# Long convolution and 2-D Fourier filter on one core: the 4096 points split as 128 by 32 in place of 64 by 64

## The chip, the cores and the metric

The kernel runs on one core of one Trainium2 chip. The core has five engines that each work through their own list of instructions: TensorE (PE in the profile; its weight loads are PEld), VectorE (DVE), ScalarE (ACT), GpSimd (POOL), and SyncE (SP), which here issues all DMAs. The metric is device time in microseconds of one execution; lower is better. Three runs of the kernel before gave 575.78, 577.08 and 578.83 us, median 577.08.

## What is computed

The input `x` has 2048 positions and 640 channels. Branch a is a long convolution: a kernel `K` of 2048 taps per channel is made from 128 complex modes and applied through transforms of 4096 points. Branch b is a two-dimensional real transform, a product with `w`, and the way back. A sigmoid gate per position mixes both.

```python
def reference(A_u, A_log_A_real, A_A_imag, A_C_real, A_C_imag, A_log_dt, A_D_skip, B_x, B_w_r, B_w_i, gate_w):
    # a: u = A_u, L = 2048
    dt = exp(log_dt)
    A = -exp(log_A_real) + 1j * A_imag
    C = (C_real + 1j * C_imag) * dt[:, None]
    P = exp((A * dt[:, None])[:, :, None] * arange(L))
    K = 2.0 * einsum("dn,dnl->dl", C, P).real
    y = irfft(rfft(u_t, 2 * L) * rfft(K, 2 * L))[:, :, :L]
    a = y.transpose + u * D_skip
    # b
    b = irfft2(rfft2(x) * (w_r + 1j * w_i))
    g = sigmoid((x * gate_w).sum(-1))
    return g * a + (1 - g) * b
```

## The kernel before, in words

**Transforms in two steps.** A transform over time is split: position n = a + 64 b, frequency in two parts as well. The first step sums over b with a small table of cosines and sines, the second over a with a table per first frequency. `POS_K` lists the 33 first frequencies that a real input needs, `NP` their number; `T.e1` is the first table, `T.w2` the second. The 640 channels are handled as four groups c of 160. All data is float32; a float32 matmul of the program is two matmul instructions in the trace.

**Where things stand.** `body` calls the parts in turn: `columns_head` and `columns` (transform u along time, write it to `u_d` in DRAM, and sum the gates), `params` (prepare the modes on DVE, ACT and POOL), `responses` (make K), `spectral` (branch b on the even time frequencies in `u_d`, result to `s3e_d`), and `convolution` (transform K, multiply by `u_d`, transform back, mix with branch b, write out).

- `stage1` is the first transform. Eight channel blocks are one step: 32 matmuls in which the data block is the weight and the table `T.e1` moves, 64 columns each, into a pair of PSUM banks; then two copies of 128x512 into `t1`, both on ACT or one of them on DVE. Groups are handled in two parts of 24 and 16 blocks (`HALVES`), so a group takes five steps; `columns` and `convolution` have four groups each.
- `stage2` is the second transform: for each first frequency two matmuls with 128x64 weights from `T.w2` and 160 moving columns from `t1`.
- The gate in `columns`: POOL builds a spread copy of the gate weights (L696), PE multiplies it with u (L704), ACT copies, and at the end DVE reduces (L719).
- `columns` writes second-transform results through `ut` to `u_d` (copies L715, half on ACT, half on DVE).
- `responses` has 40 tiles of 16 channels, in batches of five. `mags` makes exponentials (PE L919, ACT L920), `turned` sines (PE L931, ACT L932), `phases` the products on POOL (L941) and DVE (L946 to L949), and `kgen` the taps: 64 matmul instructions per tile, 128x32 weights, 64 moving columns (L962). Every two tiles go through ACT to `k_d`.
- `spectral` runs a software pipeline over nine blocks: `front` (L772 is its first DVE step), `transposes`, `channels`, `filt`, `back1`, `back2` (L856).
- `convolution`: `first` runs `stage1` on K from `k_d`. `unit` takes two pairs of frequencies: `stage2` into PSUM, two DVE products with u (L1015, L1016), two DVE sums (L1017, L1018), the inverse second step on PE (L1028), one ACT copy into `s3` (L1031). `final` sums the even branch through PE and ACT (L1043, L1054), turns `s3` by DVE's 32x32 block transposition (L1056), sums it on PE and mixes on DVE (L1059). Its buffers lie on those of `params` and `responses`, so group 0's transform of K starts when the last tile of K is made.

**What sets the order.** Nothing is issued directly: `Engine` records each call in `Plan` with its dependences, and `order` (a planner with modelled durations) chooses one order for all engines. Its weights are in `OPT`: a bias per part ("A" columns, "P" parameters, "K" responses, "F" spectral, "C" convolution) and thresholds. Each engine then works through its list in that order and waits where an operand is not ready. SP's list of DMAs is in order too: a DMA that waits for its data holds back those behind it.

Of the kernel before, what the change touches and what calls it, by code (L numbers as in the profile page):

```python
# [10 lines left out]
F32 = mybir.dt.float32  # L11
# [3 lines left out]
ALU = mybir.AluOpType  # L15
# [10 lines left out]
NP = 33  # L26
# [17 lines left out]
A_ORDER = [*range(31, -1, -1), *range(32, 64)]  # L44


def _tables():

    b = np.arange(32)
    co = np.array([np.cos(2 * np.pi * k * b / 64) for k in POS_K])  # L50
    si = np.array([-np.sin(2 * np.pi * k * b / 64) * (k not in (0, 32)) for k in POS_K])


    kr = np.stack([co, si], 1)
    kr[K0, 1] = co[32]
    e1 = np.zeros((2, 2, 2, 32, 2, 32))
    for r in range(2):
        e1[:, :, r, :, r, :] = kr[:32].transpose(1, 2, 0)[:, None]
    e1 = e1.reshape(2, 128, 64)

    e3 = np.tile(kr[:32].swapaxes(0, 1).reshape(64, 32), (2, 1))
    kr = kr[:32].reshape(64, 32)
    e3e = np.zeros((2, 32, 2, 2, 32))
    for x in range(2):
        e3e[:, :, x, x, :] = kr[32:64]
    one = np.tile(np.eye(32), (4, 1))
    c1 = np.concatenate([
        e1[0], e1[1], e3, e3e.reshape(128, 64), np.eye(128), one,
        np.repeat([-1.0, 1.0], 64)[:, None], np.repeat([1.0, -1.0], 64)[:, None],
        np.full((128, 1), HALF_PI)], 1)  # L70
# [1040 lines left out]
```

## Time and profile before

| what | value |
| --- | --- |
| runs of the kernel | 575.78, 577.08, 578.83 us |
| the profiled execution | 575.73 us |
| its span in the profile | 573.9 us |
| mean granted clock of TensorE | 0.944 |
| DMA moved | 79.44 MB, mean 138 GB/s |
| instructions in the trace | 21303 |

The span is what the profiler saw between the first and the last instruction; 1.8 us of the execution's own time lie around it. Busy time is the union of an engine's instructions. Matmuls are pipelined, so the duration of one contains filling and draining; what many cost together is read from a run of them on the timeline (start of the run, length of the run, count). The chain that ended last covers only the last ten us here, so the span is read by stretches of it.

### The profile page before, as it was taken

The numbers are of one execution on the slowest core, as the hardware profiler recorded it, in microseconds if no ns is written. First come the engines' busy times: TensorE is split into PE (matmuls) and PEld (weight loads), VectorE is DVE, ScalarE is ACT, GpSimd is POOL, SyncE is SP. The second block draws the span as 40 slices with busy tenths as digits, with TensorE's granted clock in tenths as the row PEclk, the third lists the DMA queues.
The fourth block names the chain that finished last, engine by engine and source line by source line (L and its number), as shares of the span: only waits on it lengthen the run. The fifth ranks groups of instructions, "written<-read, shape, count | busy, mean of one in ns | idle before, by whom it ended". The sixth has DMA issues, their size and how long they took to land. (4 is left out here: it accounts for less than half of the span.)

```text
span 573.9 us, 21303 instructions
## 1 busy us (share of the span) xinstructions
PE 489.1 (85%) x9428; PEld 339.9 (59%) x9428; DVE 423.5 (74%) x763; ACT 356.3 (62%) x553; POOL 178.8 (31%) x159
## 2 busy tenths in 40 slices
PE   4858998978899988999999998786798889979973
PEld 3647775655675755665765765464666666655530
DVE  7298533766999999999899886650736868928975
ACT  3443349579598796787888869653274544753550
POOL 2156412613824738355456470900000000000000
PEclk9798999988899999899999999985899999989996
DMA  8825871863106051443221202168556342452522
GB/s 317 300 95 198 297 276 47 272 223 102 48 21 201 11 163 42 128 157 98 94 66 49 74 32 74 44 237 320 145 188 170 106 146 88 153 139 74 148 104 91
DMA packets 36773, 79.44 MB, mean 138 GB/s; under 512 B 3717, under 2 KB 21001, under 8 KB 35913
## 3 DMA queue, kind: packets, MB, share of 16 engines
q1 hardware_dynamic: 36680, 78.08, 41.6%
q8 instruction: 74, 1.21, 0.9%
q14 instruction: 19, 0.15, 0.1%
HBM read 49.40 MB, written 28.67 MB: 136 GB/s over the span
## 5 line engine op out<-in xcount | busy, mean ns | idle before, releaser
L941 POOL TENSOR_TENSOR sb<-sb 128x512 f32<-128x512 f32 x80 | 105.9, 1351 | 79.2 <-ACT sb L932 66.9
L658 PE MATMUL ps<-sb 128*64 128x160 f32 x1056 | 98.3, 324 | 9.3 <-DVE sb L1016 3.6
L658 PEld LDWEIGHTS ps<-sb 128*64 128x64 f32 x1056 | 75.0, 141 | 32.2 <-issue 12.0
L931 PE MATMUL ps<-sb 52*128 52x512 bf16 x480 | 69.0, 381 | 13.8 <-DVE sb L949 8.0
L645 PE MATMUL ps<-sb 64*64 64x64 f32 x2560 | 56.0, 237 | 28.0 <-ACT sb L648 9.7
L1031 ACT COPY sb<-ps 128x640 f32<-128x640 f32 x32 | 42.0, 1312 | 55.3 <-PE ps L1028 47.8
L648 ACT COPY sb<-ps 128x512 f32<-128x512 f32 x65 | 45.3, 770 | 45.9 <-PE ps L645 45.2
L645 PEld LDWEIGHTS ps<-sb 64*64 64x64 f32 x2560 | 49.3, 149 | 39.1 <-ACT sb L648 13.5
L1015 DVE TENSOR_TENSOR sb<-ps,sb 128x640 f32<-128x640 f32 (+1 forms) x36 | 28.0, 779 | 49.8 <-PE ps L658 49.6
L920 ACT ACTIVATE sb<-ps 128x1024 f32<-128x1024 f32 (+1 forms) x80 | 62.2, 836 | 2.2 <-PE ps L919 2.1
L1028 PE MATMUL ps<-sb 64*64 64x160 f32 x1024 | 49.1, 310 | 9.2 <-issue 3.3
L1028 PEld LDWEIGHTS ps<-sb 64*64 64x64 f32 x1024 | 36.7, 136 | 25.3 <-issue 9.9
L932 ACT ACTIVATE ps<-ps 128x1024 f32<-128x1024 f32 x40 | 40.5, 1013 | 17.4 <-PE ps L931 13.2
L949 DVE TENSOR_TENSOR sb<-sb,ps 128x512 f32<-128x512 f32 x80 | 51.1, 679 | 0.0
L932 ACT ACTIVATE sb<-ps 128x1024 f32<-128x1024 f32 x40 | 41.3, 1031 | 14.0 <-PE ps L931 12.9
L931 PEld LDWEIGHTS <-sb 52*128 52x128 bf16 x480 | 25.1, 95 | 40.6 <-issue 24.4
L755 PE MATMUL ps<-sb 128*128 128x161 f32 (+3 forms) x280 | 48.3, 314 | 0.2
L962 PEld LDWEIGHTS ps<-sb 128*32 128x32 f32 x2560 | 39.4, 112 | 12.0 <-issue 8.6
L962 PE MATMUL ps<-sb 128*32 128x64 f32 x2560 | 45.9, 225 | 0.0
L946 DVE SCALAR_TENSOR_TENSOR sb<-sb,ps 128x512 f32<-128x512 f32 x40 | 27.3, 683 | 24.4 <-ACT ps L932 23.9
L755 PEld LDWEIGHTS ps<-sb 128*128 128x128 f32 (+1 forms) x280 | 39.5, 188 | 9.3 <-issue 7.2
L1043 PE MATMUL ps<-sb 64*32 64x480 f32 (+1 forms) x384 | 31.9, 709 | 6.5 <-DVE sb L1056 5.1
(129 smaller groups left out, 776.9 us busy)
## 6 DMA issues: line engine op xcount, KB each, us to landing
sb<-u_d SPq DMA_DIRECT2D x24, 640.0 KB
u_d<-sb SPq DMA_DIRECT2D x32, 320.0 KB
sb<-in_w_l SPq DMA_DIRECT2D x8, 642.0 KB
k_d<-sb SPq DMA_DIRECT2D x20, 256.0 KB
s3e_d<-sb SPq DMA_DIRECT2D x16, 320.0 KB
sb<-s3e_d SPq DMA_DIRECT2D x8, 640.0 KB
out<-sb SPq DMA_DIRECT2D x3, 1280.0 KB
sb<-k_d SPq DMA_DIRECT2D x4, 768.0 KB
```

Of the source, the lines that this page charges most:

```text
L645: T.P.matmul(p[64 * ri:64 * ri + 64, h, 64 * j:64 * j + 64], src(i + j)[l], T.e1[ri][l], start=True, stop=True)
L648: copies[h](t1v[:, h, q:q + 2 * n], p[:, h, 0:64 * n].rearrange("p (q x y) -> p q x y", x=16, y=2))
L658: T.P.matmul(p[64 * j:64 * j + 64, i, 160 * ri:160 * ri + 160], T.w2[:, x, 64 * ri:64 * ri + 64], t1[:, x // 2 if x < 32 else K0 // 2, :, ...
L755: P.matmul(p[:, 161 * i:161 * i + n], lhs(i, part), tab(i)[part][0], start=i == 0, stop=False)
L920: u = S.activation(ef[:, :, c:c + n], p[:, :, :n], AF.Exp)
L931: P.matmul(p[:, h, :], st.pp[l, zz], turns[l, v, s], start=s == 0, stop=s == 2)
L932: u = S.activation(p if o is None else o, p if o is None else p.rearrange("p h (v c) -> p h v c", v=2), AF.Sin, scale=TWO_PI)
L941: G.tensor_tensor(out=y[:, v], in0=e[:, :, 64:96], in1=sc[:, 1 - v], op=ALU.mult)
L949: V.tensor_tensor(out=xh[:, 0, h].rearrange("p d (y j) -> p d y j", y=2), in0=eh[:, h, :, 0:64].rearrange("p d (y j) -> p d y j", y=2), in ...
L962: P.matmul(st.pb[32 * r:32 * r + 32, o, :], y[:, ri, 4 * qq + JR[r], :], x[:, ri, 4 * qq + JR[r], :], start=t % 2 + qq + 1 - ri == 0, stop ...
L1028: P.matmul(q[x:x + 64, j, 160 * i:160 * i + 160], w3[l, pr + i, ri, x:x + 64], t2[l, ri, i, :], start=ri + i == 0, stop=ri + i == 2)
L1031: S.copy(s3[:, :, 2 * pr:2 * pr + 4].rearrange("p d (i j) -> p j i d", j=2), q[:, :, 0:320].rearrange("p j (i d) -> p j i d", i=2))
```

## The change

The split is now n = a + 32 b with 64 values of b and 65 first frequencies in place of 33.

- First transform: the table `T.e1` is the weight and 16 blocks of data move through it, 512 columns at a time, two matmuls per step. The outcome has frequency along partitions and position along columns; DVE turns it in 32x32 blocks straight out of the PSUM pair into `t1` (L643). The copies are gone. A group still takes five steps.
- Second transform: tables of 64x32, eight places of the PE array in place of two.
- The gate sums are 16 DVE passes over a second copy of u, laid out by position (`u_n`, eight DMAs), each with an accumulated output (L709).
- `kgen` makes 32-column taps: twice as many matmuls, half as wide.
- `back2` and the inverse step in `unit` use smaller tiles; `finish` uses fewer, larger ones. The sums in `unit` move from DVE to POOL. The PSUM banks of `convolution` are shared out anew: one pair for `stage2`, four banks for the inverse, one pair for `final`.
- In `columns` the copies to `ut` are all ACT's for groups 1 to 3.
- `params` takes two more DVE steps (the phase is brought back into one turn).
- Besides small corrections of its modelled durations, the planner has in `OPT` a bias per function and engine instead of five.

```diff
-NP = 33
+NP = 65
-OPT = {"bias": {"A": 9e3, "F": 20e3, "K": -19.5e3, "C": -14e3, "P": -1500.0}, "hold": 100.0, ...
+OPT = {"bias": {"back1.DVE": -104576, "channels.ACT": -19089, ..., "A": -213990}, "slack": ...
-HALVES = ((0, 24), (24, 16))
+HALVES = ((0, 48), (48, 32))
...
-    V.scalar_tensor_tensor(out=ph, in0=th, scalar=-0.5, in1=ph, op0=ALU.mult, op1=ALU.add)
+    V.scalar_tensor_tensor(out=ph, in0=th, scalar=1008.0, in1=ph, op0=ALU.mult, op1=ALU.add)
+    V.tensor_scalar(out=y, in0=ph, scalar1=MAGIC, scalar2=MAGIC, op0=ALU.add, op1=ALU.subtract)
+    V.tensor_tensor(out=ph, in0=ph, in1=y, op=ALU.subtract)
...
-def stage1(T, pair, src, q0, nq, t1, copies):
+def stage1(T, pair, src, q0, nq, t1):
+    t1v = t1.rearrange("p (h q) k -> p h (q k)", h=2)
+    for i in range(0, nq, 16):
+        p = pair()
+        with block(T.R):
+            for h in range(2):
+                l = slice(64 * h, 64 * h + 64)
+                T.P.matmul(p[:, h], T.e1[l], src(i)[l], start=True, stop=True)
+        q = 32 * (q0 + i)
+        T.V.transpose(t1v[:, :, q:q + 512], p)
         yield
-def stage2(T, p, t1, pr, i):
+def stage2(T, ps, t1, g):
+    with block(T.R):
+        for ri in range(2):
+            o = slice(160 * ri, 160 * ri + 160)
...
+            for j in range(4):
+                for s in range(2):
+                    l = slice(64 * s, 64 * s + 64)
+                    T.P.matmul(ps[s][32 * j:32 * j + 32, o], T.w2[l, 4 * g + j, 32 * ri:32 * ri + 32], t1[l, :, 4 * g + j], start=True, stop=True)
...
-                (V.tensor_copy if i else S.copy)(ut[:nl, i], src)
+                (S.copy, V.tensor_copy if c == 0 else S.copy)[i](ut[:nl, i], ps[i][:nl, 0:320])
...
+    for i in range(0, 16, 2):
+        un = T.un()
+        Y.dma_start(un, A["u_n"][:, i:i + 2])
+        for j in range(2):
+            V.scalar_tensor_tensor(out=T.gx, in0=un[:, j], scalar=1.0, in1=T.gw, op0=ALU.mult, op1=ALU.mult, accum_out=T.gate[:, 0, i + j:i + j + 1])
...
+                for e, p in enumerate(pp):
+                    P.matmul(p[64 * hf:64 * hf + 64, 0:320], w3[64 * e:64 * e + 64, kk, :], st.qq[j][64 * e:64 * e + 64, 320 * hf:320 * hf + 320], start=True, stop=True)
...
-            for qq in range(4):
-                o = 4 * (t % 2) + qq
+            for q in range(8):
                 for ri in (1, 0):
-                    for r in (0, 1, 2, 3):
-                        P.matmul(st.pb[32 * r:32 * r + 32, o, :], y[:, ri, 4 * qq + JR[r], :], x[:, ri, 4 * qq + JR[r], :],
+                    for h in range(2):
+                        for s in range(2):
+                            o = 64 * h + 32 * s
+                            P.matmul(st.pb[o:o + 32, 8 * (t % 2) + q, :], x[:, ri, 8 * h + q, 32 * s:32 * s + 32], y[:, ri, 8 * h + q, :],
...
-    rings = [(Banks(R, [5], 2), Banks(R, [3], 2))] * 2 + [(Banks(R, [6], 2), Banks(R, [2, 4], 2))] * 2
+    fin, two, four = Banks(R, [0], 2), Banks(R, [2], 2), Banks(R, [4], 4)
+    begin = Banks(R, [3, 5], 2)
...
-        V.tensor_tensor(out=t2[:nl, 0, :n], in0=ma[:nl, :n, 0], in1=ma[:nl, :n, 1], op=ALU.subtract)
-        V.tensor_tensor(out=t2[:nl, 1, :n], in0=mb[:nl, :n, 0], in1=mb[:nl, :n, 1], op=ALU.add)
+        G.tensor_tensor(out=t2[:nl, 0, :n], in0=ma[:nl, :n, 0], in1=ma[:nl, :n, 1], op=ALU.subtract)
+        G.tensor_tensor(out=t2[:nl, 1, :n], in0=mb[:nl, :n, 0], in1=mb[:nl, :n, 1], op=ALU.add)
...
+                for j in range(4):
+                    for s in range(2):
+                        l, o = slice(32 * j, 32 * j + 32), slice(64 * s, 64 * s + 64)
...
+                        P.matmul(q[o, j, 0:160], w3[l, 2 * g + s, ri, :], t2[l, ri, s, :], start=ri == 0, stop=ri == 1)
+        S.copy(s3[:, :, 4 * g:4 * g + 4].rearrange("p d j -> p j d"), q[:, :, 0:160])
...
                 for s in range(2):
-                    for x in range(2):
-                        for j in range(2):
-                            l, o = slice(64 * j, 64 * j + 64), 64 * x + 32 * s
-                            P.matmul(p[o:o + 32, j], w(l, x), src(l, x, 8 * s + a, n), start=True, stop=True)
+                    for j in range(2):
+                        P.matmul(p[64 * s:64 * s + 64, j], w(j), src(j, 8 * s + a, n), start=True, stop=True)
```

The planner's order moves with it. First the head of SP's list, before and after. Names: `in_cr_l`, `in_ci_l`, `in_la_l`, `in_ai_l`, `in_ld_l`, `in_t_pc`, `in_t_r` belong to the parameters, `in_t_c` and `in_t_w` are the transform tables, `in_u_l` and `in_u_n` the two copies of u, `in_gw_l` the gate weights; behind them stand the sizes.

```order
L548 DMA sb<-in_cr_l 128x640
L548 DMA sb<-in_ci_l 128x640
L671 DMA sb<-in_u_l 128x512
L517 DMA sb<-in_t_c 128x128
L671 DMA sb<-in_u_l 128x1024 x2
L519 DMA sb<-in_t_c 128x259
L677 DMA sb<-in_gw_l 128x160
L691 DMA sb<-in_t_w 128x768 x2
L694 DMA sb<-in_u_l 128x1536
```

```order
L545 DMA sb<-in_cr_l 128x640
L545 DMA sb<-in_ci_l 128x640
L542 DMA sb<-in_ld_l 128x5
L545 DMA sb<-in_ai_l 128x640
L545 DMA sb<-in_la_l 128x640
L549 DMA sb<-in_t_pc 128x640
L546 DMA sb<-in_t_r 128x3840
L549 DMA sb<-in_t_pc 128x640 x3
L552 DMA sb<-in_ds_l 1x320 x2
L692 DMA sb<-in_u_l 128x1536
L689 DMA sb<-in_t_w 128x704 x3
L707 DMA sb<-in_u_n 128x1280
```

All parameters moved ahead of u and of the tables; `in_t_c` with the first table, third to fourth place before, now comes behind the second load of `in_u_n`.

Second, DVE's list where the convolution begins, before and after. L847 and L831 are the last step of the spectral part, L967 the skip term of a finished block of K, L1015 and L1016 (L999 and L1000 after) the two products of a unit.

```order
L847 TENSOR_TENSOR sb<-sb 128x2x160
L967 TENSOR_TENSOR sb<-sb 128x8
L1015 TENSOR_TENSOR sb<-ps,sb 128x640
L1016 TENSOR_TENSOR sb<-ps,sb 128x640
L1017 TENSOR_TENSOR sb<-sb 128x320
L1018 TENSOR_TENSOR sb<-sb 128x320
```

```order
L643 STREAM_TRANSPOSE sb<-ps 128x2x512 x4
L827 TENSOR_TENSOR sb<-ps,sb 64x161 x4
L643 STREAM_TRANSPOSE sb<-ps 128x2x512
L831 TENSOR_TENSOR sb<-sb 64x2x160
L999 TENSOR_TENSOR sb<-ps,sb 32x320
L1000 TENSOR_TENSOR sb<-ps,sb 32x320
L999 TENSOR_TENSOR sb<-ps,sb 128x640
L1000 TENSOR_TENSOR sb<-ps,sb 128x640
```

The five transpositions of group 0 stand between the end of K and the first product, the last spectral steps among them, and the sums are gone from this list. Further up, DVE's list has ten tiles of `phases` ahead of the first step of `front`, five before.

More of the change, by code (lines that the diff above doesn't have):

```diff
@@ L279, in call @@
             out = k["out"] if "out" in k else a[0]
-            ins = [x for x in aps if x is not out]
+            ins = [x for x in aps if x is not out and x is not k.get("accum_out")]
             n = max(x.free_size() for x in (out, *ins) if x.space != DRAM)
@@ L553, in params @@
     V.memset(T.dsk, 0.0)
[L554 to L555 removed]
+    for r in range(2):
+        Y.dma_start(T.dsk[64 * r + 31:64 * r + 32], A["ds_l"][r:r + 1])
     x, kf, r, h = t5(), t5(), t5(), t5()
@@ L694, in columns @@
                 Y.dma_start(T.us[-1][:, 0:n], A["u_l"][c + 1, :, q0:q0 + n])
-            zz = T.az()[:, 0:n]
-            G.tensor_tensor(out=zz, in0=T.one.unsqueeze(1).broadcast_to([128, n, 32]),
-                            in1=T.gw[:, c, q0:q0 + n].unsqueeze(2).broadcast_to([128, n, 32]), op=ALU.mult)
-            for _ in stage1(T, pair, lambda q: u[:, q, :], q0, n, t1, (S.copy, V.tensor_copy if c else S.copy)):
-                pass
-            p = bank()[:, 0:64]
-            with block(R):
-                for q in range(n):
-                    x = 32 * (q % 4)
-                    P.matmul(p[x:x + 32], zz[:, q, :], u[:, q, :], start=q < 4, stop=q >= n - 4)
@@ L718, in columns @@
-    p = bank()[:, 0:64]
-    V.tensor_reduce(out=T.lr, in_=T.lg.rearrange("p x a -> p a x"), axis=mybir.AxisListType.X, op=ALU.add)
-    with block(R):
-        for r in range(4):
-            P.matmul(p[32 * r:32 * r + 32], T.one, T.lr, start=True, stop=True)
-    for r in range(4):
-        l, a = slice(32 * r, 32 * r + 32), 8 * r
-        V.tensor_copy(T.gate[l, 0, 0:8], p[l, 31 - a:23 - a if r < 3 else None:-1])
-        V.tensor_copy(T.gate[l, 0, 8:16], p[l, 32 + a:40 + a])
+            for _ in stage1(T, pair, lambda i: u[:, i:i + 16, :].rearrange("p q a -> p (q a)"), q0, n, t1):
+                pass
@@ L873, in spectral @@
         if old:
-            for j in range(old.nl // 64):
+            for j in range(old.nj):
                 back2(old, n - 2, j)
@@ L881, in spectral @@
                 front(n + 1, sts[n + 1])
-            for j in range(prv.nl // 64):
+            for j in range(prv.nj):
                 back1(prv, j)
```

288 lines of the change are left out of this document (128 added, 160 removed).

## The prediction

> **What bounds the kernel now.** I read the first part of the page (busy time of each engine), then the table of stretches. Its columns are: stretch and length in us; busy us and instructions of PE, PEld, DVE, ACT and POOL; granted clock; DMA share and GB/s. I cut the span where the timeline shows the work change.
>
> ```profile
> PE 489.1 (85%) x9428; PEld 339.9 (59%) x9428; DVE 423.5 (74%) x763; ACT 356.3 (62%) x553; POOL 178.8 (31%) x159
> core 0: us, PE busy (x) PEld busy (x) DVE busy (x) ACT busy (x) POOL busy (x), PEclk, DMA share, GB/s
> 0.00:98.00 98.00, 74.15 (x2034) 61.31 (x2034) 56.02 (x92) 44.75 (x80) 32.70 (x27) 0.93 0.63 220
> 98.00:121.00 23.00, 22.08 (x508) 15.27 (x497) 16.27 (x31) 15.57 (x24) 11.45 (x10) 1.00 0.75 250
> 121.00:383.00 262.00, 238.58 (x3650) 158.68 (x3646) 228.13 (x414) 205.85 (x313) 134.05 (x123) 0.96 0.28 90
> 383.00:401.00 18.00, 12.79 (x340) 10.08 (x340) 0.60 (x1) 7.95 (x12) 0.57 (x1) 0.70 0.92 349
> 401.00:552.00 151.00, 133.51 (x2801) 92.05 (x2802) 109.70 (x204) 75.83 (x111) 0.00 (x0) 0.97 0.45 130
> 552.00:574.00 22.00, 8.00 (x112) 2.48 (x111) 12.79 (x26) 6.33 (x16) 0.00 (x0) 0.78 0.30 120
> 250.00:300.00 50.00, 48.23 (x802) 32.91 (x801) 46.95 (x79) 41.35 (x63) 27.18 (x26) 1.00 0.32 99
> ```
>
> No single engine bounds the whole program. I name the rows A to F. In C, where the kernel responses (K) and the two-dimensional filter (F) run together, DVE is busy 228 of 262 us, and 94% in its steady part (last row). In E, the convolution, PE leads with 133.5 of 151 us, DVE has 109.7, POOL nothing. In D almost nobody works. In A, DVE is busy 56 of 98 us. So a change can win in A, D and E by freeing PE or ordering work better; C follows DVE's load.
>
> The starts that I use (start us, duration us, engine, line, what; in brackets the idle time before and who ended it):
>
> ```profile
> 3.76 0.49 DVE L594 TENSOR_SCALAR sb<-sb 128x640 int32<-128x640 int32 x1 [2.20 <-DMA sb<-in_cr_l]
> 69.97 0.35 SPq L583 DMA_DIRECT2D pp_d<-sb  x1
> 83.35 1.28 ACT L920 ACT_TABLE_LOAD   x1 [1.08 <-PE ps L919]
> 97.64 0.69 DVE L946 SCALAR_TENSOR_TENSOR sb<-sb,ps 128x512 f32<-128x512 f32 x1 [0.96 <-ACT ps L932]
> 102.47 0.69 DVE L946 SCALAR_TENSOR_TENSOR sb<-sb,ps 128x512 f32<-128x512 f32 x1 [0.96 <-ACT ps L932]
> 120.90 0.83 DVE L772 TENSOR_TENSOR sb<-sb 128x640 f32<-128x640 f32 x1 [1.15 <-DMA sb<-u_d]
> 390.85 2.41 PE L645 MATMUL ps<-sb 64*64 64x64 f32 x64 [1.11 <-ACT sb L648]
> 401.05 0.82 DVE L1015 TENSOR_TENSOR sb<-ps,sb 128x640 f32<-128x640 f32 x1 [17.45 <-PE ps L658]
> ```
>
> DVE could work from 3.76, but K's first step on DVE stands at 97.64 and F's first at 120.90. Alone, K takes 4.8 us a tile (97.64 to 102.47). In D, DVE idles 17.45 us while PE and ACT hand one PSUM pair to and fro (L645 waits for L648).
>
> **The change, part by part.** Groups (line, engine, operation, count, busy us, mean ns, idle before):
>
> ```profile
> L946 DVE SCALAR_TENSOR_TENSOR sb<-sb,ps 128x512 f32<-128x512 f32 x40 | 27.3, 683 | 24.4 <-ACT ps L932 23.9 <-PE ps L962 0.3
> L947 DVE TENSOR_TENSOR sb<-sb,ps 128x512 f32<-128x512 f32 x40 | 27.1, 678 | 0.0
> L949 DVE TENSOR_TENSOR sb<-sb,ps 128x512 f32<-128x512 f32 x80 | 51.1, 679 | 0.0
> L648 ACT COPY sb<-ps 128x512 f32<-128x512 f32 x65 | 45.3, 770 | 45.9 <-PE ps L645 45.2 <-PE ps L658 0.7
> L648 DVE COPY sb<-ps 128x512 f32<-128x512 f32 x15 | 10.3, 693 | 13.9 <-PE ps L645 13.8
> L715 DVE COPY sb<-ps 128x320 f32<-128x320 f32 x32 | 15.3, 488 | 22.6 <-PE ps L658 19.3 <-issue 2.4 <-ACT sb L715 0.7
> L1056 DVE STREAM_TRANSPOSE sb<-sb 128x1024 f32<-128x1024 f32 x20 | 23.8, 1222 | 2.7 <-ACT sb L1031 2.7
> L1017 DVE TENSOR_TENSOR sb<-sb 128x320 f32<-128x320 f32 (+1 forms) x36 | 16.6, 461 | 1.7 <-PE ps L1028 1.6
> L1018 DVE TENSOR_TENSOR sb<-sb 128x320 f32<-128x320 f32 (+1 forms) x36 | 16.7, 466 | 0.2
> L608 DVE SCALAR_TENSOR_TENSOR sb<-sb 128x640 f32<-128x640 f32 x1 | 0.8, 818 | 0.0
> L621 DVE SCALAR_TENSOR_TENSOR sb<-sb 128x640 f32<-128x640 f32 x1 | 2.0, 2011 | 0.0
> L846 POOL TENSOR_TENSOR sb<-sb 128x320 f32<-128x320 f32 x17 | 16.5, 970 | 40.7 <-DVE sb L843 40.7
> L856 PE MATMUL ps<-sb 128*128 128x320 f32 x68 | 25.9, 488 | 0.8 <-DVE sb L815 0.6
> ```
>
> And on PE, weight loads and matmuls of small tiles, with one unit of the convolution:
>
> ```profile
> 251.39 2.01 PE L962 MATMUL ps<-sb 128*32 128x64 f32 x128
> 419.67 1.04 PE L1043 MATMUL ps<-sb 64*32 64x480 f32 x16
> 545.09 0.18 PEld L1043 LDWEIGHTS ps<-sb 64*32 64x32 f32 x16 [0.24 <-DVE sb L1017]
> 409.46 0.82 DVE L1016 TENSOR_TENSOR sb<-ps,sb 128x640 f32<-128x640 f32 x1
> 410.33 1.38 PE L658 MATMUL ps<-sb 128*64 128x160 f32 x16 [0.38 <-DVE sb L1016]
> 411.64 1.33 PE L1028 MATMUL ps<-sb 64*64 64x160 f32 x32
> 411.83 0.82 DVE L1015 TENSOR_TENSOR sb<-ps,sb 128x640 f32<-128x640 f32 x1 [0.76 <-PE ps L658]
> 300.13 2.55 POOL L941 TENSOR_TENSOR sb<-sb 128x512 f32<-128x512 f32 x2
> 300.68 1.27 DVE L949 TENSOR_TENSOR sb<-sb,ps 128x512 f32<-128x512 f32 x2
> ```
>
> *First transforms.* Forty steps stay. A step had 64 instructions of 64 columns on four tiles; now it has four of 512 on two, the same column time, so I count no gain on PE. Two ACT copies (L648) become one DVE transposition of 1024 elements out of PSUM. The trace has that only out of SBUF, 1.22 us (L1056). The two L648 copies of 512 read the same amount out of PSUM in 2 x 0.69 = 1.39. I take 1.22, the same operation; the lower end is one straight pass at L608's pace, 1024/640 x 0.82 = 1.31, so 1.2 to 1.4 is near; above that nothing in the trace bounds it, which is a rival.
>
> *Second transforms.* Sixteen instructions of 128x64 take 1.38 us. Now 32 of 64x32 do the same on eight tiles. From L1043: its second eight start about 0.4 us behind the first, 50 ns for 480 columns, so 17 ns for 160: 32 x 17 + 0.27 of filling = 0.81. Bounds: 0.75 and no gain (1.38). I take 0.81, 0.57 less per pair; 33 in E: -19 us of PE. *Inverse step* L1028, 1.33 with 64x64 tiles, becomes 32x64 tiles, eight instead of four: again 0.81, 32 times, -17. *End sums* (L1043): the response half uses 128x64 tiles, two at a time: 8 x 0.4 / 2 + 0.2 = 1.8 against 1.04, nine calls in E: +7. L856 becomes four 64x64 tiles at once: about half of its 25.9 less fill, -9 in C.
>
> *Responses.* 128 instructions of 32 columns replace 64 of 64. L962 ran 128 in 2.01 us, 14 ns apart with 0.22 of drain. The weight loads of 545.09 stand 5 ns apart (0.18 less one load of 0.11, over 15), so issue allows about 7, half of 14. Ends: 7 ns (nothing lost) and 14 (5120 x 7 = +36 us of PE). I take 7, nearest to equal column time.
> The Trainium skill, "TensorE: Matmul & The Clock Gate", section "Wait — 56ns, not 53.3ns?", says that start-to-start never drops below about 25 ns however few the columns. L962 is already at 14, over four tiles, so the trace disagrees for tiles; by the page the sum would have 5120 x 18 = 92 us more of PE, and that is a rival below.
>
> *Gate sums.* Sixteen DVE passes of 640, 0.82 each (L608), 2.01 if the port is contested (L621): 13 us, up to 32. They replace L696 on POOL and L704 on PE. Their input is read a second time, 16 rows of 640 per partition (5.2 MB); at A's 220 GB/s 24 us of DMA beside other work. *Copies*: 24 of 32 L715 leave DVE for ACT, -11.7.
>
> *Products to POOL.* L1017 and L1018 leave DVE, 33.3 us. POOL needs 0.97 each (L846), 1.94 a unit beside 3 us of cycle, and had nothing in E: hidden, though 1 us longer before the inverse matmul, which is queued on PE ahead of the next step. If not hidden it is 36 us. While POOL ran 300.13 to 302.68, DVE's L949 with one PSUM operand kept its 0.64 each, and E's DVE steps are of that kind.
>
> *Order.* On SP's queue, all parameters now stand ahead of u and the tables. Ten K tiles stand before F's first step on DVE, five before. DVE rows up to the last parameter part add up to 51 us at these durations, so from 3.8 to 55; write and read back about 5; from the table load to the first K step 97.64 - 83.35 = 14.3, of which 2.6 were other copies, so 12: K starts at 72 instead of 97.6. Ten tiles at 4.6 to 4.8 bring F to 118. DVE has to be busy 102 us by then: 72.3 (A and B) - 10.3 - 11.2 - 1.6 + 20 x 1.22 + 13.1 + five tiles of 2.64 (L946, L947, L949 over 40) + 1.3; it fits.
>
> Sum by stretch:
> - A and B: 121 to 118, **-3**.
> - C: DVE 228.1 - 13.2 (five tiles) - 1.3 = 213.6; at the share it had, 0.87: 245, **-17**. PE: 238.6 - 17.6 (five tiles at 3.5) - 9 = 212, still under it.
> - D: five transpositions, 6.1, a load and a first step: 9 for 18, **-9**.
> - E: DVE 109.7 - 32.4 + 15 x 1.22 = 95.6; PE 133.5 - 29 = 104.5. DVE's share was 0.73 with PE ahead and 0.94 in C's steady part. The second transforms have one PSUM pair, so stage and multiply alternate (409.46 to 411.83 shows it), though other DVE steps fill the gap: 0.80 gives 119.5, **-31.5**; the ends are 101 and 131.
> - F: **+1**, two-tile end sums.
>
> Together -59.5. The profiled execution took 575.7 (span 573.9), near the median of 577.1; it becomes 516, and the median **518**.
>
> **Rivals.** *E keeps its share and K's small matmuls gain nothing* (14 ns). For: one PSUM pair, L962. Against: half the columns. C has 33 us of slack on PE, so 27 more would cost about 10; with E's 131: 540. *The clock drops.* In D the granted clock was 0.70 with PE busy 12.8 of 18; E's PE falls from 88% to 87%, so I don't expect it; a third of E at half clock adds 30: 548. *K does not start early* because its loads queue behind u_d writes that wait for PE: C keeps five tiles, 538. *A floor of 25 ns per matmul*: thirty tiles in C x 128 x 18 ns = 69, (212 + 69)/0.97 = 290 for C, 45 more: 565. *Slower*: the transposition out of PSUM runs at a fraction of SBUF's pace. A and B hide 12 us, so 40 x (t - 1.22) - 12 eats the gain from t = 3.0 us; at 4 us, 617. Against it: no other DVE step is slower from PSUM.
>
> **How the numbers follow.** Forecast (486 to 535) 0.72; the first three rivals (528 to 550) 0.17; below 486 (E at 0.95 and F at 110) 0.04; the floor 0.03; slow transposition 0.04. The range 486 to 550 takes in the bounds of E and of the small matmuls. A measurement tells 0.5% from no change: faster 0.94, same 0.02, slower 0.04.
>
> **What will show it.** Right: the transposition group near 1.22 us; first K step near 72; F's first near 118; DVE's idle before the first product under 3 us instead of 17; the convolution near 120 us with DVE at 80%; L1014 blocks near 0.8. Wrong: K's matmuls 14 ns apart, a clock under 0.9 in E, DVE waiting for POOL's results through PE, or F waiting for u_d after 130.

## The result and the profile after

The changed kernel took 605.93 us (median of four runs, 604.03 to 609.15), the kernel before 577.96 beside it (575.78 to 579.62): a ratio of 1.049, 95% interval 1.043 to 1.055. It is 5% slower where 518 us was forecast.

The first part of the page, and the table of stretches cut at A to F as in the prediction (F's first step now stands at 161, so B is split in two rows):

```profile
PE 490.7 (81%) x10140; PEld 260.4 (43%) x10140; DVE 440.7 (73%) x716; ACT 319.0 (53%) x502; POOL 228.7 (38%) x223
core 0: us, PE busy (x) PEld busy (x) DVE busy (x) ACT busy (x) POOL busy (x), PEclk, DMA share, GB/s
0.00:86.00 86.00, 55.14 (x748) 23.75 (x748) 59.78 (x93) 30.41 (x53) 21.71 (x19) 0.96 0.75 261
86.00:121.00 35.00, 29.02 (x884) 14.14 (x882) 25.88 (x43) 22.71 (x32) 12.69 (x10) 0.95 0.46 153
121.00:161.00 40.00, 28.41 (x948) 14.71 (x941) 13.78 (x23) 26.80 (x42) 12.66 (x10) 0.93 0.41 142
161.00:421.00 260.00, 221.46 (x5170) 147.86 (x5169) 219.10 (x375) 176.48 (x271) 121.98 (x112) 0.91 0.28 83
421.00:438.00 17.00, 13.18 (x78) 5.63 (x68) 9.19 (x13) 3.76 (x10) 0.75 (x1) 0.79 0.81 248
438.00:582.00 144.00, 133.08 (x2294) 51.62 (x2292) 102.31 (x150) 54.17 (x85) 58.91 (x72) 0.98 0.54 146
```

Read against the forecast: K's first step on VectorE stands at 85.9 (72 forecast, 97.6 before). A and B end at 161 (118; 121), with VectorE idle for 62 of those 161 us. C is 260 (245; 262 before) although ten response tiles are done ahead of it instead of five. D is 17 (9; 18). E is 144 in this row and 139.6 from the first product to the last, which is how the row of before was cut (119.5; 151); TensorE is busy 92% of the row. Single places of the timeline (start, duration, engine, line, what, count, in brackets the idle time before and who ended it):

```profile
85.93 0.69 DVE L933 SCALAR_TENSOR_TENSOR sb<-sb,ps 128x512 f32<-128x512 f32 x1 [5.34 <-issue]
161.37 0.83 DVE L754 TENSOR_TENSOR sb<-sb 128x640 f32<-128x640 f32 x1 [0.34 <-DMA sb<-u_d]
414.29 1.33 PE L950 MATMUL ps<-sb 128*32 128x32 f32 x129
419.18 1.96 PE L950 MATMUL ps<-sb 128*32 128x32 f32 x127 [3.55 <-issue]
480.96 0.80 PE L1014 MATMUL ps<-sb 32*64 32x160 f32 x32
482.82 1.50 PE L658 MATMUL ps<-sb 64*32 64x160 f32 x32
493.69 3.42 PE L1025 MATMUL ps<-sb 128*64 128x480 f32 x8
```

The inverse step (L1014) takes the forecast 0.80 us on eight tiles. The second transforms (L658), on eight tiles too and with half as many columns of weights, take 1.50 instead of 0.81, and the end sums (L1025) 3.42 instead of 1.8. Before a response block (L950) TensorE stands still for 3.55 us, marked issue: it waited for nothing that the profile shows. The groups (busy us, mean ns of one, idle before and who ended it):

```profile
L643 DVE STREAM_TRANSPOSE sb<-ps 128x1024 f32<-128x1024 f32 x40 | 49.4, 1240 | 19.6 <-PE ps L641 18.8
L658 PE MATMUL ps<-sb 64*32 64x160 f32 x2048 | 97.0, 483 | 10.8 <-DVE sb L1000 4.6 <-issue 3.6 <-DVE sb L643 2.3
L950 PE MATMUL ps<-sb 128*32 128x32 f32 x5120 | 59.2, 205 | 18.4 <-issue 18.2
```

The transposition out of PSUM is 1.24 us, as forecast. The response matmuls are followed by 18.2 us of issue idle time that L962 did not have.

### The profile page after: what moved, and what is told of

The parts are those of the page before. It is cut to its first block, busy times and chain, and to the rows that moved or that the text cites. A ratio compares the mean times of both kernels' runs of the same rounds, so it can differ in the third digit from the quotient of the medians.

```text
span 603.6 us, 22720 instructions
## 1 busy us (share of the span) xinstructions
PE 490.7 (81%) x10140; PEld 260.4 (43%) x10140; DVE 440.7 (73%) x716; ACT 319.0 (53%) x502; POOL 228.7 (38%) x223
## 5 line engine op out<-in xcount | busy, mean ns | idle before, releaser
L658 PE MATMUL ps<-sb 64*32 64x160 f32 x2048 | 97.0, 483 | 10.8 <-DVE sb L1000 4.6
L1015 ACT COPY sb<-ps 128x640 f32<-128x640 f32 x32 | 40.9, 1279 | 82.7 <-PE ps L1014 82.7
L950 PE MATMUL ps<-sb 128*32 128x32 f32 x5120 | 59.2, 205 | 18.4 <-issue 18.2
L641 PE MATMUL ps<-sb 64*128 64x512 f32 x160 | 50.7, 714 | 27.8 <-DMA sb<-in_u_l 21.5
L658 PEld LDWEIGHTS ps<-sb 64*32 64x32 f32 x2048 | 41.5, 119 | 66.0 <-DVE sb L1000 23.1
L950 PEld LDWEIGHTS ps<-sb 128*32 128x32 f32 x5120 | 53.6, 117 | 34.2 <-issue 32.1
L643 DVE STREAM_TRANSPOSE sb<-ps 128x1024 f32<-128x1024 f32 x40 | 49.4, 1240 | 19.6 <-PE ps L641 18.8
L1001 POOL TENSOR_TENSOR sb<-sb 128x320 f32<-128x320 f32 (+1 forms) x36 | 30.0, 834 | 83.7 <-DVE sb L999 81.4
L830 POOL TENSOR_TENSOR sb<-sb 128x320 f32<-128x320 f32 (+1 forms) x17 | 16.2, 952 | 110.0 <-DVE sb L827 110.0
L1025 PE MATMUL ps<-sb 64*64 64x480 f32 (+3 forms) x192 | 48.7, 720 | 8.5 <-DVE sb L1038 4.2
L701 ACT COPY sb<-ps 128x320 f32<-128x320 f32 (+1 forms) x60 | 23.6, 431 | 52.2 <-PE ps L658 43.3
L738 PE MATMUL ps<-sb 128*128 128x161 f32 (+4 forms) x280 | 48.3, 315 | 1.7 <-issue 1.3
L738 PEld LDWEIGHTS ps<-sb 128*128 128x128 f32 (+2 forms) x280 | 38.8, 185 | 10.6 <-issue 7.2
L999 DVE TENSOR_TENSOR sb<-ps,sb 128x640 f32<-128x640 f32 (+1 forms) x36 | 28.1, 780 | 19.4 <-PE ps L658 14.1
```

The source lines that it names most:

```text
L641: T.P.matmul(p[:, h], T.e1[l], src(i)[l], start=True, stop=True)
L643: T.V.transpose(t1v[:, :, q:q + 512], p)
L658: T.P.matmul(ps[s][32 * j:32 * j + 32, o], T.w2[l, 4 * g + j, 32 * ri:32 * ri + 32], t1[l, :, 4 * g + j], start=True, stop=True)
L738: P.matmul(p[:, 161 * i:161 * i + n], lhs(i, part), tab(i)[part][0], start=i == 0, stop=False)
L950: P.matmul(st.pb[o:o + 32, 8 * (t % 2) + q, :], x[:, ri, 8 * h + q, 32 * s:32 * s + 32], y[:, ri, 8 * h + q, :], start=t % 2 + q + 1 - ri ...
L1015: S.copy(s3[:, :, 4 * g:4 * g + 4].rearrange("p d j -> p j d"), q[:, :, 0:160])
```

## The experiments

Three theories, which do not exclude each other. **1**: the second transforms and end sums read their moving operand with 32 floats between elements, and that is slow. **2**: the new order of work delays F. **A**: the doubled number of response matmuls is more than TensorE's instruction supply can follow. Unless said otherwise a kernel keeps every instruction of the changed kernel in its order (the planner's list written out), so that only the edit differs.

This table has all whole kernels: the median, then from VectorE's groups the first step of F, the time from there to the first product of the convolution (C and D), and from the first to the last product (E). The median is over all runs of a kernel, 4 to 10; the three columns behind it come from its one profiled execution. The four runs of the changed kernel alone spread over 5 us, so differences of a few us between rows say little.

| kernel | median us | F starts | C and D | E |
| --- | --- | --- | --- | --- |
| before | 577.96 | 120.9 | 280.1 | 150.9 |
| forecast | 518 | 118 | 254 | 119.5 |
| changed | 605.93 | 161.4 | 277.1 | 139.6 |
| old order | 628.01 | 122.3 | 331.5 | 142.0 |
| contiguous table | 602.38 | 164.1 | 273.2 | 137.8 |
| both contiguous | 601.84 | 163.6 | 274.5 | 131.8 |
| padded to 33 | 597.99 | 158.5 | 274.6 | 137.7 |
| wide weights | 593.18 | 164.7 | 260.9 | 138.3 |
| padded and wide | 596.29 | 161.1 | 271.2 | 139.3 |
| pairs | 591.86 | 155.9 | 277.4 | 132.6 |
| pairs, both arrays | 584.22 | 155.7 | 274.2 | 123.1 |
| sums back on VectorE | 610.49 | 163.4 | 278.2 | 144.2 |
| short gate sums | 604.44 | 161.7 | 278.2 | 139.5 |
| pairs both, wide | 574.65 | 154.6 | 265.3 | 122.4 |
| pairs both, spread | 588.23 | 164.1 | 273.8 | 122.3 |
| pairs both, loads first | 596.20 | 166.7 | 278.6 | 124.0 |
| pairs both, old response matmuls | 561.98 | 152.3 | 256.5 | 125.3 |
| the same, copies back | 563.48 | 153.9 | 258.0 | 125.1 |
| the same, old order | 617.59 | 136.4 | 317.6 | 136.6 |

**Reads by stride, alone.**

```diff
+x[:, 0:160 * s].rearrange("p (d k) -> p d k", k=s)[:, :, s // 2]   # moving operand, s = 1 ... 64
```

> Only isolated blocks, nothing of the kernel's work (the output is zeros): matmuls of 160 columns on eight 64x32 tiles, four-bank 128x64 tiles and full 128x128 tiles, with a moving operand whose successive elements lie 1, 2, 4, 8, 16, 31, 32, 33 or 64 floats apart; then the copy on ACT and the transposition on VectorE with strided and with contiguous results. Theory 1 (a stride of 32 floats, 128 bytes, halves the moving operand's rate): on the eight tiles strides 1 and 2 run about 17 ns apart, stride 32 about 43 ns apart, and the 128x64 tiles lose at stride 32 too. Rival (eight tiles of 64 rows by 32 columns share something and never run together): about 43 ns apart at every stride. For stride 33 Theory 1 leaves open whether only powers of two are slow (17 ns) or every stride over some size (43 ns).

Groups for strides 1, 2, 4, 32, 33 and 64 on eight tiles (384 instructions each):

```profile
L539 PE MATMUL ps<-sb 64*32 64x160 f32 x384 | 7.3, 297 | 2.3 <-issue 2.3
L541 PE MATMUL ps<-sb 64*32 64x160 f32 x384 | 7.9, 303 | 3.6 <-issue 3.6
L543 PE MATMUL ps<-sb 64*32 64x160 f32 x384 | 14.5, 463 | 0.7 <-issue 0.7
L551 PE MATMUL ps<-sb 64*32 64x160 f32 x384 | 21.3, 630 | 0.0
L553 PE MATMUL ps<-sb 64*32 64x160 f32 x384 | 14.4, 465 | 0.0
L555 PE MATMUL ps<-sb 64*32 64x160 f32 x384 | 29.9, 792 | 0.0
```

Busy time over 384 gives 19, 21, 38, 55, 38 and 78 ns an instruction. Theory 1 holds (32 floats cost 55 ns, more than the 43 expected), the rival (eight tiles never run together) falls; 32 and 64 floats are worse than 33.

**Contiguous table; both arrays contiguous.**

```diff
-T.V.transpose(t1v[:, :, q:q + 512], p)
+T.V.transpose(t1.rearrange("p k (h q) -> p h q k", h=2)[:, :, q0 + i:q0 + i + 16], p...)   # t1 is [32, 160]
```

> The array between the first and second transforms is kept with the 160 channels next to each other for each frequency, so that the second transforms read a contiguous moving operand; order of all instructions as in the changed kernel. Theory 1 (stride): a block of second transforms takes 0.8 us instead of 1.50, E falls from 144 to about 121 (33 blocks x 0.7, all on the chain stage, multiply, stage), the time from 606 to 575-585. Rival (eight small tiles never run together): block stays 1.50, time 606 within 3. Theory 2 (the order is what costs): E may shrink, but F still starts after 155 and C still takes 250 or more. The transposition now writes with a stride of 640 bytes; if VectorE is slowed by that, it shows as more than 1.24 us each.

> As the run before, and the array between the inverse step and the end sums is kept the same way. Theory 1: the response half of the end sums falls from 3.42 us to about 1.8 per 480 columns (E and F: 12 calls, some 15 us of PE), ACT's copy into that array from 1.28 to below 1.0 us; the time is 8-15 below the run before, 562-575. Rival (the end sums are slow because only two tiles run at once): 3.42 stays, the time within 3 of the run before.

Groups of the first of the two:

```profile
L643 DVE STREAM_TRANSPOSE sb<-ps 128x1024 f32<-128x1024 f32 x40 | 76.4, 1938 | 14.0 <-PE ps L641 9.9
L658 PE MATMUL ps<-sb 64*32 64x160 f32 x2048 | 61.6, 346 | 15.0 <-DVE sb L643 4.2
```

TensorE gained 35 us (97.0 to 61.6), but VectorE's transposition, now writing 640 bytes apart, went from 1.24 to 1.94 us and lost 27. The times, 602.38 and 601.84, missed their ranges and are not clear of the changed kernel's (ratios to the kernel before of 1.051 for both, against 1.049): most of the cost changed engines. The second kernel does the same in the end sums, where E does fall, from 137.8 to 131.8. The granted clock before F was lower in both as well, 0.85 and 0.81 against 0.95.

**Old order.**

```diff
-OPT = {"bias": {"back1.DVE": -104576, ...
+OPT = {"bias": {"A": 9e3, "F": 20e3, "K": -19.5e3, "C": -14e3, "P": -1500.0}, ...
```

> The changed kernel with the planner's old numbers for the order; everything else as changed. Theory 2 (the new order costs the time before F): F's first step comes at 118-125 instead of 161, C grows by the five to ten response tiles that are no longer done ahead (to 270-280), and the time falls by 15-30 to 576-590. Rival (what F loses at its start is had back later, the order is worth nothing or helps): 600-625.

628.01, above even the rival's range: F starts at 122, as theory 2 said, but C and D take 54 us more. The theory falls; the new order gains 22 us.

**Supply of instructions, alone.**

```diff
+for b in range(16): k32(b)   # 32 weight columns; then k64; then both again beside large loads
```

> Isolated blocks again, nothing of the kernel's work (the output is zeros): eight-tile matmuls at strides 1 and 3, 128x64 tiles two at a time at strides 1 and 32; then 16 response tiles' worth of matmuls of 32 columns, once with 32 weight columns (128 instructions a tile on four tiles) and once with 64 (64 instructions on two tiles), and 24 of each again while large loads run; then VectorE's transposition into layouts of several strides and ACT's copy at strides 1 to 33. Theory A (PE's instructions come too slowly for such a stream): with 32 weight columns idle time marked issue of 0.3 us or more a tile appears, at least while the loads run, and with 64 columns it is gone. Rival: no idle time in either, and the gaps in the kernel come from something else.

From the timeline, 32 weight columns without loads (312.44 to 326.30) and with them (452.36, 455.81), and groups of VectorE's transposition into 640-byte steps, steps of 16 bytes, and pairs of floats:

```profile
312.44 1.55 PE L553 MATMUL ps<-sb 128*32 128x32 f32 x159
315.93 1.28 PE L553 MATMUL ps<-sb 128*32 128x32 f32 x128 [1.94 <-issue]
319.39 1.93 PE L553 MATMUL ps<-sb 128*32 128x32 f32 x128 [2.17 <-issue]
322.84 1.93 PE L553 MATMUL ps<-sb 128*32 128x32 f32 x128 [1.52 <-issue]
326.30 1.93 PE L553 MATMUL ps<-sb 128*32 128x32 f32 x128 [1.52 <-issue]
452.36 1.93 PE L562 MATMUL ps<-sb 128*32 128x32 f32 x128 [4.81 <-issue]
455.81 1.93 PE L562 MATMUL ps<-sb 128*32 128x32 f32 x128 [1.52 <-issue]
L575 DVE STREAM_TRANSPOSE sb<-ps 128x1024 f32<-128x1024 f32 x5 | 9.4, 1886 | 0.1
L571 DVE STREAM_TRANSPOSE sb<-ps 128x1024 f32<-128x1024 f32 x5 | 9.9, 1975 | 0.2
L585 DVE STREAM_TRANSPOSE sb<-ps 128x1024 f32<-128x1024 f32 x5 | 6.3, 1251 | 0.2
```

TensorE runs 128 matmuls, then stands, again and again. Each matmul has its weight load, so a portion is 256 instructions. The first stretch has 159 matmuls, so the stops fall 31 matmuls into a tile and not at its end. A portion takes 3.4 us on average without loads (16 in 54.7 us) and 4.8 beside 274 GB/s of loads (24 in 114 us). The granted clock was 0.56 in the first case, but it does not set the pace: from one stretch to the next it is 3.46 us whether the matmuls took 1.28 us (315.93 to 319.39) or 1.93 (322.84 to 326.30). With 64 weight columns the gaps are gone but for one of 2.1 us, as theory A says. The last group shows the way out of the contiguous table's cost: with two floats side by side VectorE needs 1.25 us, no more than for whole rows, and TensorE 21 ns against 19.

**Padded to 33; wide weights; both.**

```diff
+t1 = z.pool(2, 160, 33)                                             # padded
-for s in range(2): P.matmul(... x[:, ri, 8 * h + q, 32 * s:32 * s + 32], y[...])
+P.matmul(st.pb[o:o + 64, ...], x[:, ri, 8 * h + q, :], y[...])      # wide
```

> The array between first and second transforms keeps its order but with 33 floats between channels instead of 32; all else, the order too, as changed. From the isolated blocks stride 33 costs 37 ns an instruction and stride 32 55, and VectorE writes the padded rows at its usual 1.21 us. Theory 1 (the second transforms are on the path in E and in A): block 1.2 us instead of 1.50, E 144 to about 134, F's first step 2-6 us earlier, the time 590-598. Rival (PE's blocks are hidden by VectorE's work): the time stays within 3 of 606.

> The response matmuls take 64 weight columns at once (64 instructions a tile on two 128x64 tiles) instead of two times 32; results and order as in the changed kernel. Theory A (the stream of 128 instructions a tile starves PE, 15 us of idle time before them in C, 3.5 in D, and costs 1.30 instead of 1.0 us): the idle time marked issue before these matmuls falls below 4 us, C from 260 to 235-248, the time to 585-597. Rival (C is bound by the chain through ACT and VectorE): C within 4 of 260, time 600-608.

> The two runs before together, and the array of the end sums padded to 33 as well. If both theories hold, the savings add: 575-590. If the wide weights do nothing: 590-598.

Padding gave 8 us, at the end of its range, with little of it in E (139.6 to 137.7). Wide weights gave 13; the idle time before the response blocks fell from 18.4 us to 0.1:

```profile
L949 PE MATMUL ps<-sb 128*64 128x32 f32 x2560 | 85.1, 227 | 0.1
```

But a tile's matmuls now take 64 x 33 = 2.1 us, not the 1.0 that the expectation had. The two edits together gave 596.29, no less than wide weights alone: a miss, and too noisy to read more from (the intervals of the two ratios, 1.022 to 1.043 and 1.024 to 1.043, lie on each other).

**Pairs; pairs in both arrays.** The layout that `t1` had before the change, two frequencies side by side.

```diff
-t1p = z.pool(2, 160, 32); s3p = z.pool(2, 160, 32)
+t1p = z.pool(2, 16, 160, 2); s3p = z.pool(2, 16, 160, 2)            # s3p in the second kernel
-... t1[l, :, 4 * g + j] ...
+... t1[l, 2 * g + j // 2, :, j % 2] ...
```

> The array between first and second transforms is laid out in pairs of frequencies, as it was before the change: the second transforms read every second float, VectorE writes two floats at a time, which cost 1.25 us in the isolated blocks; order of all instructions as changed. Theory 1: block 0.8 us instead of 1.50 with VectorE unburdened; 32 blocks in A save 22 us of PE, 32 in E as much. If A and B are bound by PE's own work, F's first step comes at 140-150 instead of 161; E falls from 144 to 120-128; the time 568-580. Rival for A and B (they are set by waits between the engines, not by PE's work): F's first step stays at 157 or later and the time is 580-590.

> As the run before, and the array of the end sums in pairs too (two constant tables permuted to match). The response half of the end sums falls from 3.42 us per 480 columns to about 1.8, ACT's copy from 1.28 to about 0.75. Theory 1: E another 8-12 shorter, the time 558-572. Rival (PE no longer bounds E once the second transforms are fast): within 3 of the run before.

A block of second transforms takes 0.82 us in the first kernel, the forecast's figure (first line below). VectorE's turn takes 1.38, and in the second kernel the turn of the end sums' array grows from 1.23 to 1.58 (L1038): pairs are not free for VectorE in the kernel, which the isolated blocks did not show. E falls to 132.6 and then to 123.1, against 119.5 forecast; the response half of the end sums takes 1.92 us at its fastest, near the forecast's 1.8. The other lines are of the second kernel, the last one its E:

```profile
472.32 0.82 PE L658 MATMUL ps<-sb 64*32 64x160 f32 x32 [0.36 <-DVE sb L1000]
L643 DVE STREAM_TRANSPOSE sb<-ps 128x1024 f32<-128x1024 f32 x40 | 55.1, 1381 | 19.8 <-PE ps L641 13.3 <-issue 6.2
L1038 DVE STREAM_TRANSPOSE sb<-sb 128x1024 f32<-128x1024 f32 x20 | 31.1, 1585 | 3.9 <-ACT sb L1015 3.9
429.90:553.00 123.10, 107.51 (x2242) 50.35 (x2241) 107.61 (x148) 37.20 (x79) 56.91 (x70) 0.90 0.60 158
```

F's first step moves by only 5.5 us, though TensorE has 10 us less to do before it: the rival for A and B (waits between engines) is nearer, though the granted clock before F was also lower, 0.88 for 0.95. The times, 591.86 and 584.22, are above their ranges: F started 6 to 16 us later than expected, and in the first kernel E was 132.6 instead of 120-128. C and D did not change.

**Sums back on VectorE; gate sums over 8 of 640 elements.**

```diff
-G.tensor_tensor(out=t2[:nl, 0, :n], ...
+V.tensor_tensor(out=t2[:nl, 0, :n], ...
```

> The two sums per product go back from GpSimd to VectorE; all else and the order as changed. My reading (E is bound by PE, VectorE has room but its passes lie in the chain): E 144 to 148-156, the time 608-618. Rival (the way over GpSimd lengthens each unit more than VectorE's passes would): the time falls to 592-602.

> The gate sums take 8 of their 640 elements (the gate is not what the reference has), loads and order as changed: 13 us of VectorE's 100 before F go. If they lie on the path of A and B: F's first step 5-13 earlier, the time 592-600. Rival (hidden, VectorE is idle 62 of 161 us there): F and the time within 3 of 161 and 606.

610.49 and 604.44. The way over GpSimd does not cost: without it E is 144.2 instead of 139.6 (one execution each; 148-156 was expected). The gate sums are hidden: F's first step stays at 161.7.

**What starves C: pairs and wide, spread, and the old response matmuls.**

```diff
+# spread: a tile's block in four parts, TensorE's next blocks between them
+P.matmul(st.pb[32 * r:32 * r + 32, ...], y[:, ri, d, :], x[:, ri, d, :], ...)   # old form, 64 instructions
-S.copy(kt, st.pb)
+V.transpose(kt..., st.pb...)
```

> Pairs in both arrays (as in the run with both) and 64 weight columns for the responses. If the gaps before the response matmuls (19 us in that run) are a cost of their own beside the slow reads, the time falls from 584 by 8-16 to 568-576, though each tile's matmuls take 2.1 us instead of 1.3. Rival (C is bound elsewhere): 581-588.

> Pairs in both arrays, and the 128 response matmuls of a tile are issued in four parts of 32, with TensorE's next blocks between them, so that the same instructions come less bunched; nothing else changes. Theory A (instructions arrive in portions of 256, and a tile's 256 come faster than they can be fetched): the idle time marked issue before these matmuls falls from 19 us to under 8, C with D from 274 to 258-266, the time to 568-576. Rival (the gaps only move to other blocks, since the sum of instructions is the same): issue time over all of PE stays, time within 3 of 584. Second rival (the later ends of the tiles hold up ACT and VectorE): slower than 587.

> Pairs in both arrays, and the response matmuls as before the change (32 weight columns, 64 moving columns, 64 instructions a tile instead of 128); their blocks are then turned by a transposition out of PSUM on VectorE (in place of ACT's copy) and stored in eight pieces instead of one, so that the new layout is kept. Theory A (the small matmuls cost C twice, by starved instructions and by their own time): 1.0 us a tile instead of 1.3 (or 2.1 with wide weights), no gaps, and C becomes bound by VectorE, which gets 13 us more: the time 552-566, below both kernels. Rival (C follows the chain of the tiles through ACT, GpSimd and VectorE whatever TensorE needs): 570-580, no better than the run with pairs and wide weights.

Pairs with wide weights give 574.65, within the range and level with before (ratio 0.9975, interval 0.993 to 1.002). Spreading left 16.8 of 19.1 us of idle time at these blocks, and the time rose to 588.23, past the bound of its second rival: four parts among TensorE's next blocks are no relief. C and D stayed as they were (273.8 for 274.2); the time was lost before F, which started at 164.1 instead of 155.7. The old response matmuls do away with both costs and give **561.98**, ratio 0.978 (0.974 to 0.982), below both kernels:

```profile
L957 PE MATMUL ps<-sb 128*32 128x64 f32 x2560 | 50.2, 236 | 4.1 <-DVE sb L962 3.3 <-DVE sb L936 0.5 <-POOL sb L928 0.2
0.00:152.30 152.30, 99.08 (x1942) 47.60 (x1944) 101.08 (x163) 80.41 (x125) 47.77 (x38) 0.86 0.67 219
152.30:408.80 256.50, 226.85 (x3311) 145.57 (x3308) 230.95 (x402) 168.10 (x260) 120.76 (x113) 0.92 0.35 92
408.80:534.10 125.30, 108.29 (x2241) 51.13 (x2242) 107.39 (x148) 37.14 (x79) 56.97 (x70) 0.89 0.64 173
```

C and D are 256.5, against 254 forecast, with VectorE busy 90%. The rival's 570-580 did not come. This edit also frees ACT of its copies of the response blocks (11.8 us), so alone it does not clear ACT of a part in C; the wide weights leave those copies and still shorten C and D, by 16 us without pairs and by 9 with them.

**Why F starts so late: loads first, copies back, old order again.**

```diff
+# loads first: in_t_c, in_u_l, in_t_w right behind the parameters; five transpositions earlier on VectorE
-(S.copy, V.tensor_copy if c == 0 else S.copy)[i](ut[:nl, i], ...)
+(S.copy, V.tensor_copy)[i](ut[:nl, i], ...)                         # copies back
```

> Pairs in both arrays; on the DMA queue the first column's inputs and tables go ahead of the gate's inputs and later columns (behind the parameters), and VectorE's transpositions and copies of the columns stand five places earlier. Theory 2a (A is late because TensorE cannot begin before 21.5): TensorE begins at 12-15 and F's first step comes at 146-151 instead of 155.7; the time falls by 4-10 to 574-580. Rival 2b (F's start is set by the response tiles interleaved with the columns between 86 and 150, each waiting in turn): F's first step stays at 153-157 and the time within 3 of 584.

> As the run with the old response matmuls (562.0), but every second copy of the columns' results (L701) goes back to VectorE, as before the change; order kept. Theory 2c (in A and B ACT's copies wait for TensorE in turn and hold up the sines of the response tiles behind them; VectorE idles 50 of 152 us there): F's first step 152 to 140-148, the time 550-558. Rival (the copies only block VectorE's response steps instead): F at 150 or later, time 560-570.

> As the run with the old response matmuls (562.0), with the planner's old numbers for the order. If the new order (ten response tiles ahead of F) is still worth what it was with the changed kernel (22 us): 580-590, F at 120-126 and C with D near 300. Rival (with cheap response matmuls it no longer matters, what F gains at its start it loses behind): 558-570.

With the loads first TensorE did begin at 13.27, but K's first step came at 93.5 instead of 82.5, probably since the columns now stood ahead of the parameters on VectorE (no run tests that apart), and the whole took 12 us longer, with a granted clock of 0.81 before F instead of 0.89. The copies make no difference (563.48, F at 153.9). With the old order the kernel of 561.98 takes 617.59, outside both ranges, with F at 136 instead of 120-126: the order is worth 56 us there, more than before. In its first 136 us the clock is down to 0.71 (0.86 before F with the new order), so a part of the 56 may be the clock's; no run separates it:

```profile
0.00:136.40 136.40, 86.37 (x1324) 38.44 (x1324) 81.89 (x125) 46.09 (x86) 31.74 (x27) 0.71 0.67 235
```

## Why the prediction was wrong

The span went from 516 less 1.8 forecast to 603.6, by 89 us: 43 in A and B, 23 in C and D, 20 in E and 3 in F.

**The second transforms and the end sums were mis-sized (E).** "So 17 ns for 160: 32 x 17 + 0.27 = 0.81" took the pace of L1043's contiguous rows for an operand that the change had made strided. The block took 1.50. The end sums were put at 1.8 from the same row and took 3.42. The trace of before had both cases under one line, L1043, with the same shapes and count: beside the row of 1.04 us quoted in the prediction, which reads `te` contiguously, stand rows that read `s3` at 32 floats, as this one on its timeline:

```profile
465.54 1.82 PE L1043 MATMUL ps<-sb 64*32 64x480 f32 x16
```

That row would have warned of the change's `t1`; the weight loads at 545.09 that the prediction quotes belong to another block of that kind, whose matmuls took 1.82 as well. With the layout in pairs the block is 0.82 and E 123: that eight small tiles run together was right, the term was not. That E then ends so near 119.5 is partly luck, since VectorE had 107.6 us of work in it and not 95.6, and was busy 87% of it and not 80%. Undoing the stride brings 22 us (605.93 to 584.22).

**The response matmuls had a second cost (C and D).** "I take 7, nearest to equal column time" was low for the pace inside a block: 1.33 us for 129, 10 ns, halfway to its upper end of 14. What the step missed besides is the supply of instructions. In the kernel before TensorE never stood idle ahead of a response block, so no row priced it:

```profile
L962 PE MATMUL ps<-sb 128*32 128x64 f32 x2560 | 45.9, 225 | 0.0
```

The portions of 256 arrive every 3.4 to 4.8 us, and a tile takes one whole portion in 1.3. Of the 18.2 us of issue time 15.1 fall in C, as much as C is above its forecast (260 for 245); that the two are equal proves little by itself, but with fewer response instructions C and D became 9 to 18 us shorter, unless the array was also padded (3). The 3.55 us stand in the last tile, just before D. The rival of a floor, held at 0.03, had its size (45 us in C) wrong, but a floor there is: 3.42 us over 128 is 27 ns a matmul, once a stream is longer than a portion. With half as many instructions, in their old form, C and D came to 256.5.

**The order step compared one engine only (A and B).** "DVE has to be busy 102 us by then; it fits": VectorE was busy 99.5 us before F, as worked out. TensorE was not added up. It began at 21.5, because all parameters and the gate's input stand ahead of the first column's data on SP's queue (the diff of SP's list showed that), and was busy 112.6 us: 134 even without another wait, and 16 us past the forecast of 118. K's first step came at 85.9, not 72: 14 of the 43 us. The other 29 lie in "ten tiles at 4.6 to 4.8", which was the pace of K alone, within a batch of five; beside the columns a tile took 7.5 (85.9 to 161.4), and 16.4 us of that lie between the fifth tile and the sixth, while ACT makes the exponentials of the second batch. The sum had no term for either. Lines of the changed kernel:

```profile
21.46 3.79 PE L641 MATMUL ps<-sb 64*128 64x512 f32 x8 [21.46 <-DMA sb<-in_u_l]
110.57 0.69 DVE L933 SCALAR_TENSOR_TENSOR sb<-sb,ps 128x512 f32<-128x512 f32 x1
126.96 0.69 DVE L933 SCALAR_TENSOR_TENSOR sb<-sb,ps 128x512 f32<-128x512 f32 x1 [7.21 <-ACT ps L919]
149.69 1.58 PE L658 MATMUL ps<-sb 64*32 64x160 f32 x18
153.27 0.44 SPq L749 DMA_DIRECT2D sb<-u_d  x1
160.84 0.19 DVE L955 TENSOR_TENSOR sb<-sb 128x16 f32<-128x16 f32 x1 [5.17 <-ACT sb L954]
```

Two chains end together before F's first step at 161.37. One is K's list on VectorE, whose last step (160.84) waited for ACT's copy of the last response block. The other is the columns: TensorE ends them at 151.3, F's load of `u_d` is issued at 153.3, and F's first step waits for it by 0.34 us; the sign "F waiting for u_d after 130" came. Less TensorE work, no gate sums and copies on the other engine each moved F by 0 to 6 us, and starting TensorE earlier made it later. In the kernel of 561.98, where K's list is done earlier, F waits 4.94 us for its load. Two chains of nearly equal length would explain why no single edit moved F much, but no run tests that, so which waits set the pace before F stays open. What is shown is that the order pays all the same, by 22 us in the changed kernel and by up to 56 in the best one, where part may be the clock's.

**D was right in kind, not in size.** VectorE's idle time before the first product went from 17 to pieces of at most 3.9, but K's last block, delayed by issue time, and the last spectral steps now stand there: 17, not 9.

**Right**: the transposition out of PSUM (1.24 for 1.22), the inverse step (0.80 for 0.81), `back2` (25.9 to 19.5, -6 for -9), gate sums and GpSimd's sums hidden, VectorE's load before F. The other rivals: the clock did not fall in E of the changed kernel (0.98; in C it did, 0.91 for 0.96), and K did start earlier than before, at 85.9.

## What to carry to other kernels

A change of layout has two prices, one at the engine that writes and one at the engine that reads; look up the stride of every operand that the new layout touches and price each by a row with the same stride, since a group's mean can hide two. When matmuls are made smaller, count instructions per microsecond beside column time: a stream that the old kernel never reached has no row in its profile, and a small isolated run of it costs little. When a forecast moves a stage earlier, add up every engine's work and its first load up to there, not only the engine that looked busiest.

## What the runs showed of the hardware

- TensorE's moving operand (float32, 160 columns): on eight 64x32 tiles, 1 and 2 floats apart run at full pace (19 and 21 ns), 4, 8, 16, 31 and 33 at half of it (38), 32 at a third (55) and 64 at a quarter (78). The Trainium skill, "SBUF — State Buffer", section "Door 1: The DMA port swizzle", speaks of lines of 16 bytes that need two hits each for full bandwidth and names up to four float32 as free. Two hits a line agree with the free stride of 2; at 4 the measured pace is halved, so the measurement decides.
- TensorE's instructions arrive in portions of 256: in the isolated blocks it stops after every 128 pairs of weight load and matmul. The Trainium skill, "Runtime: NRT & Kernel Launch", section "Instruction fetch mechanics", has blocks of that size and calls the cost of crossing one mostly hidden; here each portion of 128 small matmuls ends in 1.5 to 4.8 us of standing still. The Trainium skill, "TensorE: Matmul & The Clock Gate", section "Wait — 56ns, not 53.3ns?", gives about 25 ns as the least distance of small matmuls: the 10 ns measured inside a portion are below it, the 27 ns over many portions close to it.
- VectorE's 32x32 transposition of 128x1024, in the isolated blocks, writes rows of 32 or pairs of floats in 1.25 us, single floats 16 bytes or more apart in 1.9 to 2.2. In the kernel pairs took 1.38 (out of PSUM) and 1.58 (within SBUF). ACT's copy of 128x640 went from 1.28 us at 128-byte steps to 0.75 at 8-byte steps.
- The granted clock of TensorE in E was 0.98 in the changed kernel, where it was busy 130 of 140 us, and 0.90 with pairs in both arrays, where it was busy 107.5 of 123. A smaller busy share does not explain that alone: the kernel before had 0.97 at 133.5 of 151.
